# Finishing four more output tiles straight from PSUM on VectorE, with a new order of instructions

## The chip, the cores and the metric

The kernel runs on one core of a Trainium2 chip. The metric is device time in microseconds. Before the change it is 129.96 us, the median of three runs (129.57 to 130.26).

## The reference

The input `x` has 2048 rows (s) of 512 columns (d), in bfloat16. Two branches are computed from it and mixed by a gate, row by row:

```python
x = A_x
g = _sigmoid((x * gate_w).sum(-1, keepdims=True))
a = irfft2(rfft2(x) * (w_r + 1j * w_i))        # branch A, cast to bfloat16
h = einsum("bsd,df->bsf", x, w1) + b1          # branch B, f = 1792
b = einsum("bsf,fd->bsd", h * tanh(softplus(h)), w2)
return g * a + (1 - g) * b
```

Branch A is a two-dimensional Fourier filter, branch B a dense layer with the Mish activation and a second dense layer. The output has the shape of `x`.

## The kernel before

The 2048 rows are 16 tiles of 128 rows. Branch B runs in four chunks of four tiles. For a chunk, line 795 does 14 groups of four matmuls (128x512) into PSUM, line 811 applies Mish on ScalarE into `act`, and line 830 does 14 matmuls for each tile, in two halves of seven (called `mm2_t_0` and `mm2_t_1`; tile 15 is instead cut into three column pieces of 256, 128 and 128). Branch A is written as matmuls too: the transforms along the columns (line 533) and the rows (line 559), a write to a scratch tensor in HBM and a read back that regroups it (`scr<-Ybuf`, then `Abuf<-scr`), the second row step (line 656), the weights on VectorE and GpSimd (line 414, tiles `Qb` and `Zb`), the inverse row step (line 716), a second trip through scratch, and then, for every one of the 16 tiles, the inverse transforms of lines 744 and 755.

After line 755 a tile t goes through this sequence, which the change and the prediction speak of:

- line 748 (an eviction, in the trace line 409 on VectorE or 410 on ScalarE, tile `Zb`) takes the result of line 744 out of PSUM for line 755;
- `gc_t` on ScalarE (line 760) scales half of the result of line 755 by the gate; `sap_t` and `sam_t` on VectorE (line 766) scale the other half and add or subtract the first, into `Qb`;
- `sbp_t` and `sbm_t` (line 414, `Tg<-Qb`, 128x256 each) add and subtract these and leave the gated branch A in `ga`, which is the tile `Tg`. They run on GpSimd for tiles 0 to 13, and on either engine for 14 and 15;
- for tiles below `NBF`, `bev_t` evicts the second dense layer from PSUM, scaled by 1 - g (line 776 on ScalarE, line 777 on VectorE), into `xo`, and `sum_t` (line 414, `xo<-xo,Tg`, 128x512 in bfloat16) adds `ga` on VectorE. Two tiles go out in one store of 256 KB;
- for the other tiles `fin_t` (line 842) does both in one VectorE instruction: it reads PSUM, scales by 1 - g and adds `ga`. Each such tile, and each piece of tile 15, has its own store.

A PSUM bank comes free when its last reader is done. With `bev_t` that reader needs only the matmuls and the gate; with `fin_t` it needs `ga` of that tile as well.

Nothing is scheduled at run time and nothing by a cost rule: `_Graph.schedule` reads the string `ORDER`. It gives, in one list for the whole kernel, the number of the next task, the engine where a task has a choice, and the PSUM bank where a task takes one. Each engine executes its tasks in that order, and waits on semaphores for what a task depends on. So an instruction that waits holds up everything behind it on its engine. Stores and loads are issued by SyncE (the SP queue) unless the call names another queue; the first store on SyncE waits for the landing of all loads and scratch transfers. `ORDER` numbers the tasks as they are created, so other tasks mean other numbers throughout.

Of the kernel before, what the change touches and what calls it, by code (L numbers as in the profile page):

```python
# [165 lines left out]
class _Graph:  # L166
# [97 lines left out]
    "2wv2xv2l2Qa88252R22ca8n0802ya8d4262e2z52nv2Sv2U2mv3C8e2oa8Z7372p22T2qv2d30a3J8a7X17Z68r731328j48x58t23E2s7Y398"
    "f38u8p18y7a8b28o3B3G2r0f7s50e3D7j08s8c7t3I3F0t3H3K3O8h63P77k3Q3R8k3S8q3L3T3Y18g3X33W3Z3U3hv8i3M3gv7p73kv8v67q3"
    "jg8133N7uv8w3ig823a7m47la3b3lv3V3c63ng3t24F03d3e3u542v0w3f3mg7n3o3v7ra43v45g3w8N746v8O7oa3x44g47v48g3y249g3p33"
    "z4H4Ov9Z28Pa8Q73ra4Pv4Qg4G03qa4b34Tv4I4Rg9a9R54J9D69N29S404d9E4K54Sv9X08R4lv414L4A4kv4c54Ug9O9Y4Vg4e4B04M8Sa4C"
    "a4N9P44f4pv8W74W4ov8z54g64mg4ng4Da4X04h8T64rg3s904Zv4qg4i4j9J54s4Ya4t04E9Q4ua8U4vv4a9H49V09T19F28Va943959K9W9I"
# [696 lines left out]
```

## Time and profile before

| What | us |
|---|---|
| median of three runs | 129.96 |
| the profiled execution | 129.91 |
| its span (first to last instruction in the trace) | 128.2 |
| PE busy (TensorE matmuls) | 122.0 |
| DVE busy (VectorE) | 88.3 |
| ACT busy (ScalarE) | 71.4 |
| POOL busy (GpSimd) | 56.5 |

The profiled execution is the one that all durations below come from; it lies 0.05 us under the median, and 1.7 us of its time lie outside the span. PE, PEld (weight loads), DVE, ACT and POOL are the engines; SPq is SyncE's queue, ACTq the queue of ScalarE. In a row of the profile `out<-in` names the tiles, `x14` the number of instructions, and ns is the mean of one. The granted TensorE clock is full speed in this run.

### The profile page before, as it was taken

The page shows a single profiled execution, that of the slowest core. Times are in us where ns is not written, and L with a number is a line of the kernel's source. Part 1 is how long each engine was busy: PE and PEld are TensorE (multiplying, and loading weights), DVE is VectorE, ACT ScalarE, POOL GpSimd, SP SyncE. Part 2 cuts the span into 40 slices and gives each one's busy share as a digit, 9 for nine tenths or more (in the row PEclk, how much of TensorE's full clock was granted, in tenths as well). Part 3 has the DMA queues.
Part 4 walks back from the last instruction along what each step waited for, and adds up shares of the span by engine and source line. Part 5 has one row for each costly group of instructions (what it writes and reads, how often), then busy time and mean ns, then how long its engine had stood idle before and what let it go on. Part 6 is the DMA issues. An engine that isn't in the chain of part 4 may idle for free.

```text
span 128.2 us, 2701 instructions
## 1 busy us (share of the span) xinstructions
PE 122.0 (95%) x998; PEld 66.6 (52%) x1014; DVE 88.3 (69%) x175; ACT 71.4 (56%) x122; POOL 56.5 (44%) x90
## 2 busy tenths in 40 slices
PE   7999989999999999999999999999999999999970
PEld 5786445535644444444544444444457667555570
DVE  0258999897999940179787975430007979999992
ACT  1326595989988087204329455664348895955100
POOL 4000047000000045248899989700000899999930
PEclk9999999999999999999999999999999999999999
DMA  3999937599999767991000501463396000200645
GB/s 72 352 401 392 208 92 219 162 311 160 217 300 303 233 178 220 343 407 37 0 0 8 164 0 44 135 203 117 67 345 245 0 5 3 82 0 5 226 183 164
DMA packets 19293, 21.16 MB, mean 165 GB/s; under 512 B 1744, under 2 KB 15952, under 8 KB 19152
## 3 DMA queue, kind: packets, MB, share of 16 engines
q1 hardware_dynamic: 18176, 19.67, 51.4%
q10 hardware_dynamic: 816, 0.79, 1.8%
q0 software_dynamic: 288, 0.53, 1.5%
q8 instruction: 8, 0.13, 0.5%
q14 instruction: 5, 0.04, 0.1%
HBM read 13.64 MB, written 6.29 MB: 156 GB/s over the span
## 4 chain that ended last, share of the span: by engine, by line
PE 82%; DVE 13%; issue 2%; DVEq 0%; ACT 0%
PE ps L795 38%; PE ps L830 26%; DVE Qb L766 5%; DVE xo L414 5%; PE ps L430 3%; PE ps L533 3%; PE ps L559 3%; PE ps L744 2%; PE ps L716 2%; PE ps L481 2%; PE ps L755 2%; PE ps L656 2%; DVE Tg L414 1%; DVE xo L842 1%; DVE Zb L409 0%
## 5 line engine op out<-in xcount | busy, mean ns | idle before, releaser
L795 PE MATMUL ps<-xT,w_sb 128*128 128x512 bf16 (+1 forms) x237 | 53.0, 366 | 0.6 <-issue 0.3
L830 PE MATMUL ps<-w_sb,act 128*128 128x512 bf16 (+2 forms) x240 | 49.8, 354 | 0.8 <-issue 0.3
L811 ACT ACTIVATE act<-ps,b1f 128x512 bf16<-128x512 f32 x56 | 35.8, 690 | 21.0 <-PE ps L795 16.7
L830 PEld LDWEIGHTS ps<-w_sb,act 128*128 128x128 bf16 x252 | 22.8, 98 | 22.7 <-issue 0.6
L795 PEld LDWEIGHTS ps<-xT,w_sb 128*128 128x128 bf16 x240 | 22.5, 98 | 22.9 <-issue 1.4
L414 POOL TENSOR_TENSOR Tg<-Qb 128x256 bf16<-128x256 f32 x29 | 22.5, 808 | 17.8 <-DVE Qb L766 17.8
L414 POOL TENSOR_TENSOR Zb<-Qb 128x510 bf16<-128x510 f32 x16 | 19.9, 1268 | 3.1 <-DVE Qb L414 2.9
L414 DVE TENSOR_TENSOR Qb<-ps,WT 128x1024 f32<-128x1024 f32 x16 | 18.9, 1211 | 1.1 <-PE ps L656 1.1
L766 DVE SCALAR_TENSOR_TENSOR Qb<-ps,gcol,Qb 128x256 f32<-128x256 f32 x32 | 13.7, 474 | 1.7 <-ACT Qb L760 1.5
L776 ACT ACTIVATE xo<-ps,omg 128x512 bf16<-128x512 f32 x12 | 8.1, 686 | 11.0 <-PE ps L830 8.5
L580 POOL TENSOR_TENSOR gcol<-omg,gdot 128x16 f32<-128x16 f32 x1 | 2.9, 2943 | 24.7 <-DVE Tg L575 24.7
L414 DVE TENSOR_TENSOR Abuf<-ps,Tg 128x512 bf16<-128x512 f32 x16 | 10.3, 684 | 2.4 <-ACT Tg L540 2.0
L410 ACT ACTIVATE Ybuf<-ps 128x1024 bf16<-128x1024 f32 x10 | 10.0, 1021 | 2.2 <-PE ps L716 1.7
L575 DVE SCALAR_TENSOR_TENSOR Tg<-xo,Tg 128x512 bf16<-128x512 bf16 x16 | 10.5, 684 | 0.3
L409 DVE CAST Zb<-ps 128x512 bf16<-128x512 f32 x4 | 2.6, 680 | 11.6 <-PE ps L744 11.6
L379 POOL DMA_DIRECT2D xT<-act x8 | 4.0, 507 | 14.9 <-DVE act L489 14.9
L409 DVE CAST Ybuf<-ps 128x1024 bf16<-128x1024 f32 x6 | 7.3, 1221 | 2.8 <-PE ps L716 2.2
L760 ACT ACTIVATE Qb<-ps,gcol 128x256 f32<-128x256 f32 x16 | 7.1, 476 | 3.7 <-PE ps L755 3.5
L414 DVE TENSOR_TENSOR xo<-xo,Tg 128x512 bf16<-128x512 bf16 x14 | 8.7, 644 | 0.0
L410 ACT ACTIVATE Zb<-ps 128x512 bf16<-128x512 f32 x12 | 6.7, 594 | 2.1 <-PE ps L744 2.1
L409 DVE COPY xT<-ps 128x512 bf16<-128x512 bf16 (+1 forms) x5 | 2.6, 528 | 5.8 <-PE ps L481 5.8
L540 ACT ACTIVATE Tg<-ps 128x512 f32<-128x512 f32 x8 | 4.6, 599 | 2.5 <-PE ps L533 2.2
(62 smaller groups left out, 87.4 us busy)
## 6 DMA issues: line engine op xcount, KB each, us to landing
Abuf<-scr SPq DMA_DIRECT2D x8, 512.0 KB, 6.6
scr<-Ybuf SPq DMA_DIRECT2D x16, 128.0 KB, 3.8
scr<-Ybuf SPq DMA_DIRECT2D x4, 512.0 KB, 2.9
w_sb<-in_B_w_dram SPq DMA_DIRECT2D x2, 896.0 KB, 8.5
out_dram<-xo SPq DMA_DIRECT2D x7, 256.0 KB, 2.1
xo<-in_A_x_dram SPq DMA_DIRECT2D x3, 512.0 KB, 7.4
rt<-c_rt SPq DMA_DIRECT2D x2, 512.0 KB, 7.5
WT<-in_A_w_r_dram SPq DMA_DIRECT2D x7, 128.5 KB, 6.8
```

The source lines that it names most:

```text
L379: t = G.add(name, queue, issue if issue != 0.62 or queue != "pool" else 1.0, lambda e: e.dma_start(dst, src), reads=reads, writes=writes, ...
L409: fs = {"dve": ("dve", dve_dur(n, rate=rate), lambda e: e.tensor_copy(out=dst(), in_=src())), "act": ("act", act_dur(n), lambda e: e.activ ...
L410: "act": ("act", act_dur(n), lambda e: e.activation(dst(), src(), AF.Copy))}
L414: f = lambda e: e.tensor_tensor(out=o(), in0=i0(), in1=i1(), op=op)
L540: G.add(f"eg_{t}", "act", act_dur(512), lambda e, gb=gb, pa=pas[0], pv=pv: e.activation(G0[:, gb].rearrange("p t c (m s) -> p t c m s", s= ...
L575: lambda e, t=t: e.scalar_tensor_tensor(out=junk[t % 2], in0=xo[:, t, :], scalar=1.0, in1=gwb, op0=ALU.mult, op1=ALU.mult, accum_out=gdot[ ...
L760: lambda e, t=t, sl=sl, p5=p5: e.activation(gC[:, sl, :].rearrange("p (i n) -> p i n", i=2), ps[:, p5.bank, :].rearrange("p (i n) -> p i n ...
L766: lambda e, t=t, sl=sl, p5=p5, o=o, op=op: e.scalar_tensor_tensor(out=st1[:, sl, o::2, :], in0=ps[:, p5.bank, :].rearrange("p (i n) -> p i ...
L776: G.add_multi(f"bev_{t}", [("act", act_dur(512, True), lambda e: e.activation(xo[:, t, :], ps[:, pd.bank, :], AF.Copy, scale=omg[:, t:t + ...
L795: ins = e.matmul(o if c < 2 else o.rearrange("p (a t j) -> p a t j", a=4, t=4), w1_sb[:, i, 128 * ft:128 * (ft + 1)], xTp[:, i, 512 * c + ...
L811: lambda e, c=c, ft=ft, pd=pd, hb=hb: e.activation(act[:, hb, ft, :].rearrange("p (t a j) -> p t a j", t=4, a=4), ps[:, pd.bank, :].rearra ...
L830: ins = e.matmul(ps[:, pd.bank, cs_], act[:, hb, ft, 128 * tl:128 * (tl + 1)], w2_sb[:, ft, cs_], start=(ft == 0), stop=(ft == NFT - 1))
```

## The change

`NBF` falls from 14 to 10. Tiles 10, 11, 12 and 13 so lose their eviction `bev_t` and their sum `sum_t`; each gets one `fin_t` instead, and a store of 128 KB of its own in place of half of a 256 KB store. The stores of tiles 13 and 14 are issued by ScalarE's queue instead of SyncE's. The whole string `ORDER` is replaced: other order on all five engines, other PSUM banks, and other choices of engine where a task has two.

```diff
 ORDER = (
-    "0M0N0420506070P080O090A0B0U0C00010Q0D0R0E020F0G0H0I0x00yv0J0K0L0T0z30S10v037F27511151347A314v1X67K70V7B12a1Y7G"
+    "0M0450P05060708090N0A0B000C0D0U0E010O0F0G0H0I0x10yv0J0K0Q0z20L10v0R7K37501140S12v1357F6027A77G14v7L7B761Zv7C7D"
...
 )
-NBF = 14
+NBF = 10
 SHQ = ("pool", "sp", "pool", "sp")
...
                     dma(f"out{t}{part}", ov[:, t, cs_], xo[:, t, cs_], reads=[("o", t, part)],
-                        nbytes=256 * (cs_.stop - cs_.start), is_out=True, prio=PR["fin"], tail=0.6)
+                        nbytes=256 * (cs_.stop - cs_.start), is_out=True, prio=PR["fin"], tail=0.6, queue="act" if t in (13, 14) else "sp")
```

The number of matmuls is the same. Two places are shown in their order, since the next section rests on them.

The end of VectorE's program. L766 are `sap_t` and `sam_t`, `xo<-xo,Tg` the sums, `Tg<-Qb` the `sb` additions, `Zb<-ps` the evictions ahead of line 755, and L842 the `fin` instructions. First before:

```order
L766 SCALAR_TENSOR_TENSOR Qb<-ps,gcol,Qb 128x2x128 x6
L414 TENSOR_TENSOR xo<-xo,Tg 128x512 x4
L766 SCALAR_TENSOR_TENSOR Qb<-ps,gcol,Qb 128x2x128 x3
L414 TENSOR_TENSOR xo<-xo,Tg 128x512
L766 SCALAR_TENSOR_TENSOR Qb<-ps,gcol,Qb 128x2x128
L414 TENSOR_TENSOR Tg<-Qb 128x2x128 x3
L842 SCALAR_TENSOR_TENSOR xo<-ps,omg,Tg 128x512
L414 TENSOR_TENSOR xo<-xo,Tg 128x512 x2
L842 SCALAR_TENSOR_TENSOR xo<-ps,omg,Tg 128x256
L842 SCALAR_TENSOR_TENSOR xo<-ps,omg,Tg 128x128 x2
```

So three `Tg<-Qb` additions, tile 14 and the sums of tiles 13 and 12 stand just ahead of tile 15's pieces. And the same place now, still on VectorE:

```order
L842 SCALAR_TENSOR_TENSOR xo<-ps,omg,Tg 128x512
L766 SCALAR_TENSOR_TENSOR Qb<-ps,gcol,Qb 128x2x128
L414 TENSOR_TENSOR xo<-xo,Tg 128x512
L766 SCALAR_TENSOR_TENSOR Qb<-ps,gcol,Qb 128x2x128 x2
L414 TENSOR_TENSOR Tg<-Qb 128x2x128
L414 TENSOR_TENSOR xo<-xo,Tg 128x512
L766 SCALAR_TENSOR_TENSOR Qb<-ps,gcol,Qb 128x2x128 x2
L414 TENSOR_TENSOR xo<-xo,Tg 128x512
L842 SCALAR_TENSOR_TENSOR xo<-ps,omg,Tg 128x512
L766 SCALAR_TENSOR_TENSOR Qb<-ps,gcol,Qb 128x2x128 x2
L842 SCALAR_TENSOR_TENSOR xo<-ps,omg,Tg 128x512 x2
L842 SCALAR_TENSOR_TENSOR xo<-ps,omg,Tg 128x256
```

Behind the last row shown stand `fin_13` (128x512) and the two 128x128 pieces of tile 15. Two of the three `Tg<-Qb` additions on VectorE have gone to GpSimd, which has 31 of them at its end instead of 29, with `sbp_13` and `sbm_13` (tile 13's) last. The two `fin` in one row are those of tiles 11 and 12.

SyncE's queue between the regrouped loads (`xT<-act`) and the first read of scratch (`Abuf<-scr`). `WT` are the filter weights, `w_sb` here the halves of `w2`. Before:

```order
L379 DMA w_sb<-in_B_w_dram 128x7x512
L379 DMA WT<-in_A_w_i_dram 16x4112 x2
L379 DMA WT<-in_A_w_r_dram 16x4112
L379 DMA scr<-Ybuf 64x4x256
L379 DMA WT<-in_A_w_i_dram 16x4112 x2
L379 DMA scr<-Ybuf 64x4x256 x15
L379 DMA WT<-in_A_w_r_dram 16x4112
L379 DMA WT<-in_A_w_r_dram 16x16x257
L379 DMA rt<-c_rt 128x2048
L379 DMA Abuf<-scr 128x2048 x4
```

Here both halves of `w2` (the other stands further ahead) are issued ahead of all 16 writes to scratch. Now:

```order
L379 DMA scr<-Ybuf 64x4x256 x4
L379 DMA WT<-in_A_w_i_dram 16x4112
L379 DMA w_sb<-in_B_w_dram 128x7x512
L379 DMA WT<-in_A_w_i_dram 16x16x257
L379 DMA WT<-in_A_w_r_dram 16x257
L379 DMA scr<-Ybuf 64x4x256 x2
L379 DMA WT<-in_A_w_i_dram 16x4112 x2
L379 DMA scr<-Ybuf 64x4x256
L379 DMA WT<-in_A_w_r_dram 16x4112
L379 DMA scr<-Ybuf 64x4x256 x9
L379 DMA WT<-in_A_w_i_dram 16x4112
L379 DMA WT<-in_A_w_r_dram 16x4112
```

The same 16 writes and the same loads stand ahead of the read; four writes now stand ahead of the second half of `w2`, and the last weight load ahead of the read has 16 rows of 4112 elements instead of 256 rows of 257.

More of the change, by code (lines that the diff above doesn't have):

```diff
@@ L264 @@
[L264 to L268, printed above, removed]
@@ new lines @@
+    "7M771av1X1031l27H0T1m47R51Y3J0V781711n7V21ov1pv18v0W0X1A1547E1qa1c1797W7P71C0Y7S0b7T016v7N8947I7Q1b27J1G7O191E"
+    "1B8F51d0a0c1F1D1K1wv8G8A7v78360Z1N1S1T1vv8L51R273347w2821O1ev8D47U29841fv8B78M1x01ga1W1z873361L8E1y1331H2Av1r5"
+    "381U1M8J01I7f41J8C881sa2Bv20v2Cv21v1Q1V7h38K1h61P2D17x53A3C2Ea2Jv7b022a2Hv7y2318H52Iv7i2Kv2V31iv8560d2W77c8x00"
+    "e0l8I24v2gv2M10u0s2X2fv2hv2iv0p2Yv2Zv2L20g350i8l30n2G1u2u57g1k862t41t0k2av2N8m2v2Ov8y2Pv7Z62k72wv0v2Qa2b20r2j4"
+    "2xv0j7z17a2yv2l7d02nv1j2z5252mv2ca80370o0q2R22ov8r48d730a26392Sv2p52qv3B8s0h2F8p17X43E8q8j28f38k2e8g3D2d323181"
@@ new lines @@
+    "57Y2T8t68h17e2U3F8u2r8b23G2s8e0m828Z33I7j40f0t8a3H7p03K7s58c8i3O3P67t3Q3T3L3X23M3Y63R3N7q3S3hv3V7ra3gv3a7k3Z3W"
+    "3U7m13kv3b8n03jg3lv3c73t27la3ig7ua3mg4F48o3d3u67n43v42v8N03v3ng46v8v23w45g0w9T347v3e9Z64H8O44g4Ov4Pv8w7oa3x3y7"
+    "9a3f4G19U48g3o3z8Pa49g3p38Q74I3ra4Tv403qa9R04Rg4J4b34Qg4Sv414c54K14kv4Ug4L9J24d4e9S9K4A4M4N9P04Vg4W4lv8R4f4ov4"
+    "B19Q8z04pv3s8Sa9X74g54Da9F64ng4Cv4X1904mg4qg4h9404i4E4j8W54s4Ya9Y9G4rg4Zv4t14vv4ua8X959f79164a9b38Ya4w9V19W96v"
+    "9L58T24x9M9c9g8U9d45P55H05139e52a9H15Qv5974y5R48Va5Iv5S5v55334z5Av5n25T5U5J05wa9775B55K5oa5L545M505Wg9I5C5X45x"
@@ L274 @@
+    "2565Vg55925Og5p05E5Ng5y57g5Ya5D6315zA6v6J393a5f55Z45q986B658g6Kv5ga5Fg6L35r5s5h55a5c64a6R05ug6Sa6065161gA2v6M9"
+    "B2A5v5tg6T06Cv5b5Gg6O5i6Z66NA79N4A3v6aa5dg5k5j62g6p36Qg6h66U6V6qa5eg5lg9C6r55mg6D3666W9O6b0A46Yg6iaABv67ACv9p4"
+    "6s6EA8v686j69q6Pg6x16G6F9h36ya6u996z79l19m9i6t6c6Ag69g6k6Ig9t5AEv706e6d6vvA9v6Hg6Xg729A719w09z7AFv6wg6ggAD6fg9"
+    "r73gAA6m74g6l9D9j6og9EAG9u6ng9n9xA09s9v9o9k9yA1"
 )
-NBF = 14
+NBF = 10
 SHQ = ("pool", "sp", "pool", "sp")
```

9 lines of the change are left out of this document (removed).

## The prediction

> **What bounds the kernel now.** I read the page first (busy shares and the chain of waits), then the busy time by stretch, then the end of the span in order of time.
>
> ```profile
> span 128.2 us, 2701 instructions
> PE 122.0 (95%) x998; PEld 66.6 (52%) x1014; DVE 88.3 (69%) x175; ACT 71.4 (56%) x122; POOL 56.5 (44%) x90
> PE 82%; DVE 13%; issue 2%; DVEq 0%; ACT 0%
> ...
> 54.70:95.50 40.80, 40.22 (x420) 18.97 (x427) 23.15 (x33) 19.92 (x28) 24.07 (x38) 1.00 0.34 112
> 95.50:116.50 21.00, 20.84 (x190) 13.40 (x192) 18.13 (x40) 15.23 (x32) 16.10 (x22) 1.00 0.16 62
> 116.50:124.30 7.80, 7.75 (x66) 4.99 (x63) 7.80 (x15) 1.87 (x4) 6.38 (x8) 1.00 0.46 170
> 124.30:128.20 3.90, 0.00 (x0) 0.00 (x0) 1.43 (x5) 0.00 (x0) 0.00 (x0) 1.00 0.42 135
> ```
>
> In the lines by stretch the columns are length, busy PE, PEld, DVE, ACT, POOL, granted clock, DMA share and GB/s. PE is busy in 7.75 of the last 7.80 us before 124.30, and nearly as full earlier, at full clock. The change takes no matmul away, so PE cannot end much before 124.30. What is left to win is the 3.9 us behind it, and a few tenths of PE waits; what can be lost is any new wait of PE, at one to one. The end in order of time, from timelines, a group of stores, and the stores by size (KB and us from issue to landing):
>
> ```profile
> 110.05 12.82 POOL L414 TENSOR_TENSOR Tg<-Qb 128x256 bf16<-128x256 f32 x16 [0.28 <-DVE Qb L766]
> 116.51 7.79 PE L830 MATMUL ps<-w_sb,act 128*128 128x512 bf16 x62
> 118.22 0.69 ACT L776 ACTIVATE xo<-ps,omg 128x512 bf16<-128x512 f32 x1 [0.54 <-PE ps L830]
> 121.74 1.76 DVE L414 TENSOR_TENSOR Tg<-Qb 128x256 bf16<-128x256 f32 x3
> 123.42 0.74 DVE L842 SCALAR_TENSOR_TENSOR xo<-ps,omg,Tg 128x512 bf16<-128x512 f32 x1
> 124.08 0.74 DVE L414 TENSOR_TENSOR xo<-xo,Tg 128x512 bf16<-128x512 bf16 x2
> 124.74 0.99 DVE L842 SCALAR_TENSOR_TENSOR xo<-ps,omg,Tg 128x256 bf16<-128x256 f32 x3
> 126.19 0.45 SPq L379 DMA_DIRECT2D out_dram<-xo  x1
> L379 SPq DMA_DIRECT2D out_dram<-xo x7: 332/412/450, 121.4 to 126.2; - x7
> out_dram<-xo SPq DMA_DIRECT2D x1, 128.0 KB, 1.7
> out_dram<-xo SPq DMA_DIRECT2D x2, 32.0 KB, 1.6
> ```
>
> PE ends at 116.51 + 7.79 = 124.30, ScalarE at 118.91, GpSimd at 122.87, VectorE at 125.73. VectorE is late: three additions and three 128x512 instructions stand ahead of tile 15's pieces, whose matmuls are done. SyncE issues the last seven stores one by one, 412 ns each at the median, so the last goes out at 126.19, 0.46 after VectorE's end. From there to the end of the span is 128.2 - 126.19 = 2.0 us (1.6 of it until the data have landed).
>
> **The change part by part.** The durations for VectorE and GpSimd, from the groups in the stretch from 95.5 on and from single tiles (the three numbers behind a colon are shortest, median, longest in ns):
>
> ```profile
> L766 DVE SCALAR_TENSOR_TENSOR Qb<-ps,gcol,Qb 128x256 f32<-128x256 f32 x32 | 13.7, 474 | 1.7 <-ACT Qb L760 1.5 <-PE ps L830 0.2
> L414 DVE TENSOR_TENSOR xo<-xo,Tg 128x512 bf16<-128x512 bf16 x14 | 8.7, 644 | 0.0
> L409 DVE CAST Zb<-ps 128x512 bf16<-128x512 f32 x4 | 2.6, 680 | 11.6 <-PE ps L744 11.6
> L414 DVE TENSOR_TENSOR Tg<-Qb 128x256 bf16<-128x256 f32 x3 | 1.8, 637 | 0.0
> L777 DVE TENSOR_SCALAR xo<-ps,omg 128x512 bf16<-128x512 f32 x1 | 0.7, 740 | 0.0
> L842 DVE SCALAR_TENSOR_TENSOR xo<-ps,omg,Tg 128x512 bf16<-128x512 f32 x1 | 0.7, 739 | 0.0
> L414 DVE TENSOR_TENSOR xo<-xo,Tg x14: 407/636/944, 104.6 to 124.4; 128x512 bf16<-128x512 bf16 x14
> L414 DVE TENSOR_TENSOR xo<-xo,Tg x2: 409/410/412, 124.1 to 124.4; 128x512 bf16<-128x512 bf16 x2
> L766 DVE SCALAR_TENSOR_TENSOR Qb<-ps,gcol,Qb x32: 468/474/484, 98.3 to 121.3; 128x256 f32<-128x256 f32 x32
> L414 POOL TENSOR_TENSOR Tg<-Qb x29: 721/732/972, 99.3 to 122.0; 128x256 bf16<-128x256 f32 x29
> L414 POOL TENSOR_TENSOR Tg<-Qb 128x256 bf16<-128x256 f32 x29 | 22.5, 808 | 17.8 <-DVE Qb L766 17.8
> ```
>
> A sum takes 409 to 412 ns once GpSimd is done and up to 944 while it works; GpSimd's additions stretch from 721 to as much as 972. Line 766, which has one input in PSUM, stays at 468 to 484 all through. The Trainium skill, SBUF — State Buffer, section "Who interferes with whom", says that a VectorE instruction with both inputs in SBUF and a GpSimd instruction that reads SBUF exclude each other. By that rule, the trace agrees, with 944 against 409.
>
> *VectorE.* `fin` also reads one input from PSUM. Its 739 was taken with GpSimd idle; stretched as the sums are (944 - 409 = 535) it would be 1274. I take 739, because line 766 beside a busy GpSimd did not stretch. The sums that stay: at 407 to 944 each. The last two of the 14 stand behind GpSimd's end (409 and 412 ns); the other twelve share 14 x 644 - 821 = 8195, or 683 each, and I take 683 for the ten. So from 95.5 on: sums 10 x 683 - 14 x 644 = -2.19 us; four `fin` at 739, +2.96; two `Tg<-Qb` given to GpSimd, -1.27; the one L777 eviction, which in the new list stands ahead of the `Zb` casts, in the 11.6 us in which VectorE waits, -0.74; one `Zb` cast more, +0.68; two instructions fewer, each of which overlaps its neighbour by 0.08, +0.16. Sum -0.4 (ends -3.2 and +4.4, from 407 for each sum and from 944 with 1274 for each `fin`).
>
> VectorE also begins earlier. It waits for the first results of line 744:
>
> ```profile
> 95.55 1.06 PE L744 MATMUL ps<-GMs,Abuf 128*128 128x128 bf16 x16
> 96.65 1.29 DVE L409 CAST Zb<-ps 128x512 bf16<-128x512 f32 x2 [11.61 <-PE ps L744]
> ```
>
> The 16 matmuls are four tiles, some 0.22 us apart. Before, VectorE's first cast takes the fourth; the new table gives it the first, so 3 x 0.22 = 0.7 earlier. PE has as much work ahead of that point in both lists (between the last L716 group and the first L744 group, five halves of L830 and five groups of L795 in each). The 1.7 us in which line 766 waits for ScalarE can vanish or stay; I take half, 0.85. VectorE's own work would then end at 125.73 - 0.4 - 0.7 - 0.85 = 123.8. But its last piece needs PE's last matmul: 124.30 and 0.34 for the piece, and a few hundredths for the signal, 124.7. So PE would bound it.
>
> *GpSimd.* It runs from 99.27 to 122.87, idle for 1.1 of these:
>
> ```profile
> 99.27 1.41 POOL L414 TENSOR_TENSOR Tg<-Qb 128x256 bf16<-128x256 f32 x2 [16.64 <-DVE Qb L766]
> ```
>
> The other gaps are 17.8 - 16.6. Two additions more, at 0.69 after overlap, +1.4. The stretch was 29 x (808 - 732) = 2.2 us for 17 VectorE instructions of the conflicting kind; 11 are left, -0.8. Of the 1.1 idle, 0 to 0.6 goes, since VectorE feeds it more steadily: -0.3. So GpSimd ends at 122.87 + 0.3 = 123.2 (122.9 to 123.8). `fin_13` needs its last addition, and the two last pieces stand behind it: 123.25 + 0.66 + 0.26 + 0.34 = 124.5, still under 124.7; with 123.8 it is 125.1.
>
> *Stores.* SyncE's last four are now a piece of tile 15, tile 12 and two pieces. The three pieces wait for VectorE, so there is no queue of older stores left: the last piece goes out 0.3 after VectorE's end or sooner, at 125.0 instead of 126.19. The stores of tiles 13 and 14 move to ScalarE, past its last work (118.91 before); that queue's issue costs 0.65 here, from
>
> ```profile
> 0.80 1.95 ACTq L379 DMA_DIRECT2D w_sb<-in_B_w_dram  x3
> ```
>
> and tile 13's, with `fin_13` ending at 123.25 + 0.74 = 124.0, would land at 124.1 + 1.7 = 125.8, ahead of the last piece (125.0 + 1.6 = 126.6). Two more stores of 128 KB cost nothing as long as they go out ahead of that.
>
> ScalarE loses three evictions of 0.69 us, which it did in time that nobody waited for; if its waits stay the same, nothing is gained there.
>
> *The rest of the order.* One place ahead of the tail has no slack: the first read of scratch.
>
> ```profile
> 29.62 2.08 SPq L379 DMA_DIRECT2D WT<-in_A_w_i_dram  x2
> 34.38 5.73 SPq L379 DMA_DIRECT2D scr<-Ybuf  x7
> 47.93 1.79 SPq L379 DMA_DIRECT2D Abuf<-scr  x4
> 54.69 0.35 PEld L656 LDWEIGHTS ps<-Abuf,rt 64*32 64x32 bf16 x32 [0.42 <-DMA Abuf<-scr]
> ```
>
> PE waits 0.42 for it. SyncE issues DMA after DMA up to that read, some 0.65 each; in two places (2.08 for two, 5.73 for seven) an issue took about 1 us longer. The new list has the same number ahead of it. Better by more than 0.42 it cannot get; one such long issue more costs 1.0, two 2.0. I take nothing, since the count is the same.
>
> **The sum.** The last store 1.2 us earlier (126.19 to 125.0), the 2.0 behind it unchanged, PE unchanged: 129.91 - 1.2 = 128.7; I give 0.1 back for small waits of PE in a wholly new order: 128.8. The profiled execution lies 0.05 under the median, so this is a median too.
>
> **The rivals.**
>
> *Late scratch (slower).* Four scratch writes now stand ahead of the second half of `w2` and wait for evictions of lines 409 and 410, with all that follows. Each microsecond by which the read comes later is one for PE and for the end. From 1.2 it eats the gain; from 1.85 the kernel is slower by over 0.5%. With two long issues more and a wait, 2.2: 130.9. For it: no slack. Against it: same transfers, same count. 12%.
>
> *PE waits for a bank.* With `fin` the accumulators of tiles 10 to 13 stay in PSUM until the gated branch A of that tile is done. Tile 10's bank goes next to tile 15's group of line 755, ahead of which VectorE has `fin_10` in the middle of its list, and behind which PE has the last three halves of L830 and tile 15, as before the change (7.79 us). If VectorE is 1 us late there, PE ends 1 us later: 129.8. For it: VectorE is full (7.80 of 7.80). Against: the list gives `fin_10` room. 10%.
>
> *The sum was the cheaper instruction.* The Trainium skill, VectorE: DVE Perf Modes, section "Why PSUM operands drop a tier", speaks against the change: an input in PSUM keeps VectorE from its fastest modes. In the rows, a sum alone takes 410 and `fin` 739: at 410 for the four that go, VectorE's work grows by 4 x 0.33 = 1.3 where I have it at -0.4 (four sums at 410 out, the other ten unchanged at 738: -1.64 + 2.96 - 1.27 - 0.74 + 0.68 + 0.16 = +0.15). With the idle time also unchanged, VectorE ends at 125.73 + 0.15 - 0.7 = 125.2 and the last store at 125.5: 129.2; with GpSimd at its late end too, 129.4. For it: the last two sums did take 410. Against it: most of the 14 did not. 14%.
>
> **How the numbers follow.** My forecast, VectorE's tail shortened to PE's end, has 64%. About 0.5% (0.65 us) is what a measurement can tell from no change. Faster: the forecast, 64%, with most of it under 129.2. Same: the cheap sum, 14%, and the bank wait, 8 of its 10%. Slower: the late scratch, 12%, and a bank wait of over 1.9 us, 2%. The range runs from 128.2 (forecast, and the 0.42 at the scratch read gone as well) to 130.0, which takes in the bank wait and the cheap sum and leaves the late scratch out.
>
> **What would show it.** Right: PE ends within 0.3 of 124.3; GpSimd has 31 additions and ends near 123.2; four more L842 of 128x512 at about 740 beside a busy GpSimd; VectorE ends 0.4 to 0.5 after PE; the last store leaves near 125.0. Wrong: a wait of PE on `Abuf<-scr` above 1 us, idle PE ahead of line 755 in the tail, `fin` near 1270, or the last landing being ScalarE's store.

## The result, and the profile after

The changed kernel takes 128.92 us (median of 20 runs, 127.8 to 132.7) against 129.87 us for the kernel before, run beside it (median of 20, 129.24 to 131.33). The ratio is 0.9914, with a 95% interval from 0.9888 to 0.9941: faster by 0.9%, where 0.5% can be told from no change. Forecast were 128.8 us and 128.2 to 130.0. The ratio takes in the runs within 1.5% of each kernel's fastest, 15 of 20 with a median of 128.65 us and 19 of 20 with one of 129.84; the other five of the changed kernel took 129.87 to 132.71. So the runs of the changed kernel differ more among themselves than those of the kernel before; the experiments say a part of why.

The profiled execution of the changed kernel took 129.21 us, 0.3 over its median; 1.8 us lie outside its span. From the page (span, busy shares, and the engines' shares of the chain that ended last):

```profile
span 127.4 us, 2711 instructions
PE 122.2 (96%) x999; PEld 67.0 (53%) x1014; DVE 91.0 (71%) x176; ACT 67.4 (53%) x115; POOL 57.0 (45%) x92
PE 90%; DMA 6%; issue 1%; DVE 0%
```

Before, the chain that ended last was 82% PE and 13% VectorE. VectorE has gone from it (0%); what stands beside PE now is a DMA. The timeline, at the first scratch read and at the end:

```profile
47.37 0.34 SPq L379 DMA_DIRECT2D Abuf<-scr  x1
...
55.22 0.35 PEld L656 LDWEIGHTS ps<-Abuf,rt 64*32 64x32 bf16 x32 [1.12 <-DMA Abuf<-scr]
55.23 0.63 PE L656 MATMUL ps<-Abuf,rt 64*32 64x256 bf16 x32 [0.63 <-DMA Abuf<-scr]
...
117.28 7.57 PE L830 MATMUL ps<-w_sb,act 128*128 128x512 bf16 x62
...
122.16 3.08 DVE L842 SCALAR_TENSOR_TENSOR xo<-ps,omg,Tg 128x512 bf16<-128x512 f32 x6
122.32 1.41 POOL L414 TENSOR_TENSOR Tg<-Qb 128x256 bf16<-128x256 f32 x2 [0.25 <-DVE Qb L766]
...
124.89 0.90 SPq L379 DMA_DIRECT2D out_dram<-xo  x2
```

PE ends at 117.28 + 7.57 = 124.85, VectorE at 122.16 + 3.08 = 125.24, which is 0.39 behind PE, and GpSimd at 123.73. SyncE's last two issues fill 124.89 to 125.79; the last of them starts at 125.33, 0.09 behind VectorE's end. Before, that last issue started at 126.19, 0.46 behind VectorE's end and 1.89 behind PE's. VectorE and GpSimd from 95.5 on, grouped (us in all and mean ns, then idle time ahead), and in a second fence the sums alone with shortest, median and longest ns:

```profile
L766 DVE SCALAR_TENSOR_TENSOR Qb<-ps,gcol,Qb 128x256 f32<-128x256 f32 x32 | 13.7, 474 | 0.4
L414 DVE TENSOR_TENSOR xo<-xo,Tg 128x512 bf16<-128x512 bf16 x10 | 7.4, 761 | 0.0
L842 DVE SCALAR_TENSOR_TENSOR xo<-ps,omg,Tg 128x512 bf16<-128x512 f32 x5 | 3.6, 737 | 0.0
L409 DVE CAST Zb<-ps 128x512 bf16<-128x512 f32 x5 | 3.4, 687 | 8.6 <-PE ps L744 8.6
...
L414 POOL TENSOR_TENSOR Tg<-Qb 128x256 bf16<-128x256 f32 x31 | 23.4, 787 | 17.2 <-DVE Qb L766 17.1
```

```profile
L414 DVE TENSOR_TENSOR xo<-xo,Tg x10: 415/844/947, 102.7 to 120.0; 128x512 bf16<-128x512 bf16 x10
```

The single instruction takes 737 ns beside a busy GpSimd, as it did alone. The idle time of line 766 has gone from 1.7 to 0.4 us. The ten sums that stay are not cheaper than before but dearer (761 against 644).

**One mark to measure from.** PE's first L656 group, which reads the scratch, starts at 54.69 before and at 55.23 after. Before:

```profile
54.69 0.63 PE L656 MATMUL ps<-Abuf,rt 64*32 64x256 bf16 x32
```

PE's end lies 69.61 us behind it before and 69.63 after. In twelve of the fourteen traces of this study (five of the old order, seven of the new) PE's end is 69.61 to 69.63 behind that mark; the other two are the old order with the single instruction, told of below. So the mark splits a run in two: what happened ahead of it, which differs from trace to trace (the mark lies at 54.0 to 54.7 us in the old order and at 53.6 to 56.1 in the new), and the end, where PE's path is the same to a few hundredths. By the mark, before and after:

| us behind the first L656 matmul | before | after |
|---|---|---|
| PE's end | 69.61 | 69.63 |
| VectorE's end | 71.04 | 70.02 |
| last store issued | 71.50 | 70.10 |
| end of the span | 73.5 | 72.2 |

The end is 1.3 us shorter. The medians of all runs differ by only 0.95, those of the runs in the ratio by 1.2. So a median run of the changed kernel seems to lose 0.1 to 0.3 us ahead of the mark; this is a difference of medians and is read from no single trace.

### The profile page after: what moved, and what is told of

Same layout as the page of the kernel before. It is cut to its first block, busy times and chain, and to the rows that moved or that the text cites. A ratio compares the mean times of both kernels' runs of the same rounds, so it can differ in the third digit from the quotient of the medians.

```text
span 127.4 us, 2711 instructions
## 1 busy us (share of the span) xinstructions
PE 122.2 (96%) x999; PEld 67.0 (53%) x1014; DVE 91.0 (71%) x176; ACT 67.4 (53%) x115; POOL 57.0 (45%) x92
## 4 chain that ended last, share of the span: by engine, by line
PE 90%; DMA 6%; issue 1%; DVE 0%
PE ps L795 37%; PE ps L830 33%; DMA Abuf<-scr 6%; PE ps L430 3%; PE ps L533 3%; PE ps L744 3%; PE ps L755 3%; PE ps L559 3%; PE ps L481 2%; PE ps L656 2%; PE ps L716 2%; DVE xo L842 0%; PE ps L673 0%; PE ps L499 0%; PE ps L675 0%
## 5 line engine op out<-in xcount | busy, mean ns | idle before, releaser
L830 PE MATMUL ps<-w_sb,act 128*128 128x512 bf16 (+2 forms) x242 | 49.8, 354 | 1.0 <-issue 0.6
L830 PEld LDWEIGHTS ps<-w_sb,act 128*128 128x128 bf16 x252 | 22.7, 98 | 22.7 <-issue 0.8
L414 POOL TENSOR_TENSOR Tg<-Qb 128x256 bf16<-128x256 f32 x31 | 23.4, 787 | 17.2 <-DVE Qb L766 17.1
L766 DVE SCALAR_TENSOR_TENSOR Qb<-ps,gcol,Qb 128x256 f32<-128x256 f32 x32 | 13.7, 474 | 0.4
L409 DVE CAST Ybuf<-ps 128x1024 bf16<-128x1024 f32 x7 | 8.6, 1222 | 4.3 <-PE ps L716 3.8
L410 ACT ACTIVATE Ybuf<-ps 128x1024 bf16<-128x1024 f32 x9 | 9.2, 1032 | 4.6 <-PE ps L716 3.5
L776 ACT ACTIVATE xo<-ps,omg 128x512 bf16<-128x512 f32 x9 | 6.1, 686 | 10.1 <-PE ps L830 9.9
L409 DVE CAST Zb<-ps 128x512 bf16<-128x512 f32 x5 | 3.4, 687 | 8.6 <-PE ps L744 8.6
L414 DVE TENSOR_TENSOR xo<-xo,Tg 128x512 bf16<-128x512 bf16 x10 | 7.4, 761 | 0.0
```

The source lines that it names most:

```text
L409: fs = {"dve": ("dve", dve_dur(n, rate=rate), lambda e: e.tensor_copy(out=dst(), in_=src())), "act": ("act", act_dur(n), lambda e: e.activ ...
L410: "act": ("act", act_dur(n), lambda e: e.activation(dst(), src(), AF.Copy))}
L414: f = lambda e: e.tensor_tensor(out=o(), in0=i0(), in1=i1(), op=op)
L766: lambda e, t=t, sl=sl, p5=p5, o=o, op=op: e.scalar_tensor_tensor(out=st1[:, sl, o::2, :], in0=ps[:, p5.bank, :].rearrange("p (i n) -> p i ...
L776: G.add_multi(f"bev_{t}", [("act", act_dur(512, True), lambda e: e.activation(xo[:, t, :], ps[:, pd.bank, :], AF.Copy, scale=omg[:, t:t + ...
L830: ins = e.matmul(ps[:, pd.bank, cs_], act[:, hb, ft, 128 * tl:128 * (tl + 1)], w2_sb[:, ft, cs_], start=(ft == 0), stop=(ft == NFT - 1))
```

## The experiments

In the expectations for the old order the mark was put at the second L656 group, 0.23 us later; all figures below are from the first. In kernels with an inserted line the numbers of later lines are a few higher (L657 and L658 are L656).

**Does the single instruction carry the gain?** First the new order with evictions and sums back:

```
-                    G.add(f"fin_{t}_{part}", "dve", ...)
+                    if t in (10, 11, 12, 13):
+                        evict_b(t, pd)                  # on ScalarE
+                        tt(f"sum_{t}", ..., engs=("dve",))  # where fin stood
+                    else:
+                        G.add(f"fin_{t}_{part}", "dve", ...)
```

> The changed kernel in its new order, but tiles 10 to 13 again take an eviction (on ScalarE, as soon as the matmuls are done) and a sum on VectorE where the single instruction stood. My theory (order and queue carry the gain): sums beside a busy GpSimd take as long as the single instruction (761 against 737 ns), so nothing moves: ratio to before 0.990 to 0.993. Rival (the single instruction carries the gain): ratio 0.997 or more. Second rival (ScalarE's four evictions of 0.69 us delay what VectorE waits for): 0.3 to 0.7 us slower than the changed kernel, with idle time of line 766 behind ScalarE back at over 1 us.

Measured: 128.54 us, ratio 0.990 (0.9873 to 0.9928). Timeline:

```profile
54.28 0.63 PE L657 MATMUL ps<-Abuf,rt 64*32 64x256 bf16 x32
...
116.34 7.57 PE L831 MATMUL ps<-w_sb,act 128*128 128x512 bf16 x62
...
124.47 0.46 SPq L380 DMA_DIRECT2D out_dram<-xo  x1
```

PE ends at 123.91 (69.63 behind the mark) and the last store goes out at 124.47 (70.19, against 70.10 with the single instruction). Nothing is lost without it.

My rival in the prediction was that the sum is the cheaper instruction, since a sum alone takes 410 ns and the single instruction 739. The Trainium skill has a rule for this (VectorE: DVE Perf Modes, "Why PSUM operands drop a tier"): an input in PSUM keeps VectorE from its fastest modes. It decided nothing here. The four sums of tiles 10 to 13 in this run:

```profile
113.98 0.54 DVE L415 TENSOR_TENSOR xo<-xo,Tg 128x512 bf16<-128x512 bf16 x1
...
121.42 1.28 DVE L415 TENSOR_TENSOR xo<-xo,Tg 128x512 bf16<-128x512 bf16 x2
...
123.31 0.43 DVE L415 TENSOR_TENSOR xo<-xo,Tg 128x512 bf16<-128x512 bf16 x1 [0.22 <-POOL Tg L415]
```

They took 536, 410, 945 and 426 ns, 2.3 us against 2.9 for four single instructions, so on VectorE they were the cheaper form. The 0.6 us does not arrive: in both kernels VectorE's last piece waits for PE's last matmul and ends 0.39 behind it. Beside a busy GpSimd much of a sum's advantage goes: the ten sums of the changed kernel take 761 ns in the mean and up to 947. The Trainium skill, SBUF — State Buffer, "Who interferes with whom", says for two inputs in SBUF that they contend with a GpSimd instruction that reads SBUF. My expectation (the same time either way, because a sum takes as long as the single instruction) was right in the time and wrong in the reason.

Then the old order with the single instruction put where the sums stood:

```
-                    if t < NBF or (t < NT - 1 and part == 0):
+                    if (t < NBF and t not in FIN) or (t < NT - 1 and part == 0):
...
-                if t < NBF:
+                if t < NBF and t not in FIN:
                     evict_b(t, pd)
```

with `FIN = (10, 11, 12, 13)`, sums of these tiles left out of the list, and PSUM banks assigned anew.

> The kernel before, every engine in its old order, but tiles 10 to 13 finished by one L842 instruction at the places where their sums stood (their evictions go; PSUM banks are reassigned so that PE need not wait; stores as before). My theory (the order and the stores carry the gain, the single instruction as such is worth nothing): the last two sums took 410 ns each behind GpSimd's end and become 740 each, so VectorE's tail grows by 0.66 us, less 0.2 for the sum of tile 10 that took 944; the kernel comes out 0.3 to 0.7 us slower than before, near 130.4. Rival (the single instruction carries the gain): 0.5 to 1.0 us faster, near 129.1.

Measured: 130.39 us, ratio 1.0069 (1.0035 to 1.0102). The waits of the run, then its timeline:

```profile
PE ps L745 <- DVE Qb L767: 1.0, 1, 1.0
```

```profile
54.56 0.63 PE L657 MATMUL ps<-Abuf,rt 64*32 64x256 bf16 x32
...
117.89 7.79 PE L831 MATMUL ps<-w_sb,act 128*128 128x512 bf16 x62
...
125.74 1.80 SPq L380 DMA_DIRECT2D out_dram<-xo  x4
```

Slower by what I expected, but not only for my reason. Tile 11's accumulator, held until `fin_11`, keeps the bank that tile 11's L744 group had before; the groups behind it move to other banks, and tile 15's L744 group gets one that VectorE has not yet read empty, so PE waits 1.0 us. PE ends at 125.68, 71.1 behind the mark instead of 69.6. (0.3 of these 1.5 us are there already at the first L744 matmul.) That is my rival of the bank wait, in the place of another tile. So the same without tiles 11 and 13, `FIN = (10, 12)`, whose accumulators are filled only behind that place:

> As the run before, but only tiles 10 and 12 take the single L842 instruction; with two accumulators held instead of four, no PSUM bank has to be reused early (PE waited 1.0 us for one at L744 in the run with four). My theory: PE has no new wait; the sum of tile 10 (944 ns) becomes 740, that of tile 12 (410 ns, behind GpSimd's end) becomes 735, so VectorE's end and the last store come 0.1 to 0.3 us later, measured from the first L656 matmul in the trace (71.27 us before); ratio 1.000 to 1.003. Rival (the bank wait was harmless and the single instruction itself cost the half microsecond): 0.4 us or more later, ratio 1.004 or more. Second rival (the single instruction saves time where no bank is short): 0.3 us earlier, ratio 0.997.

Measured: 129.76 us, ratio 1.0003 (0.9977 to 1.003). Timeline:

```profile
54.19 0.63 PE L657 MATMUL ps<-Abuf,rt 64*32 64x256 bf16 x32
...
123.88 1.65 DVE L843 SCALAR_TENSOR_TENSOR xo<-ps,omg,Tg 128x512 bf16<-128x512 f32 x4
```

No wait of PE at tile 15's L744 group is left. VectorE's end is at 125.53, 71.3 behind the mark, 0.3 later than before. Half of this is not the single instruction's: PE is 0.15 later from the first L744 matmul on, and so is its end. The other 0.15 is the single instruction's price at the end of the old order, where a sum runs behind GpSimd's end at 410 ns; and for tile 11 it holds a PSUM bank that the old order needs. It is worth nothing in the new one.

**Is the queue of stores the gain?** The old order, with the stores of tiles 12 and 13 (one transfer) and 14 in ScalarE's queue:

```
-    dma(f"out{t}", ..., is_out=True, prio=PR["fin"], tail=0.6)
+    dma(f"out{t}", ..., is_out=True, prio=PR["fin"], tail=0.6, queue="act" if t == 13 else "sp")
...
-    dma(f"out{t}{part}", ..., is_out=True, prio=PR["fin"], tail=0.6)
+    dma(f"out{t}{part}", ..., is_out=True, prio=PR["fin"], tail=0.6, queue="act" if t == 14 else "sp")
```

> The kernel before with nothing changed but the queue of two stores: those of tiles 12 and 13 (one store) and tile 14 go out in ScalarE's queue. My theory: SyncE then holds only the three pieces of tile 15 at the end, and the last piece goes out at VectorE's end plus 0.1 to 0.2 (125.85 to 125.95) instead of 126.19, so 0.2 to 0.35 us are gained, near 129.6. Rival (the queue of stores was the whole loss at the end): 0.8 to 1.0 us gained, near 129.0. Second rival (the end hangs on VectorE alone): nothing, 129.87.

Measured: 129.75 us, ratio 0.9999 (0.9974 to 1.0024). My 0.2 to 0.35 is not there. Timeline:

```profile
54.37 0.63 PE L656 MATMUL ps<-Abuf,rt 64*32 64x256 bf16 x32
...
124.44 0.99 DVE L842 SCALAR_TENSOR_TENSOR xo<-ps,omg,Tg 128x256 bf16<-128x256 f32 x3
124.94 1.46 SPq L379 DMA_DIRECT2D out_dram<-xo  x3
```

Tile 15's first piece ends at 124.9 and SyncE takes it at once. The other two follow at the queue's own pace, and the last goes out at 125.81: 71.44 behind the mark, 0.06 better than before. Three pieces that come out of VectorE in 1 us take SyncE 1.46 us, whatever else has left its queue.

The same two stores put back into SyncE's queue in the new order:

```
-   ..., tail=0.6, queue="act" if t in (13, 14) else "sp")
+   ..., tail=0.6)
```

> The changed kernel with only the stores of tiles 13 and 14 put back into SyncE's queue, at the places that the order gives them. My theory: SyncE must issue tile 13's store when its last instruction ends (124.6), then tile 12's and the two last pieces at 0.4 us each, so the last goes out near 125.8 instead of 125.33: 0.3 to 0.5 us slower than the changed kernel, a ratio to before of about 0.995. Rival (the queue is worth nothing, since VectorE's last piece sets the end): same as the changed kernel, ratio 0.991. Second rival (the queue is the whole gain): ratio 1.00.

Measured: 129.46 us, ratio 0.9975 (0.9934 to 1.0017). Timeline:

```profile
54.19 0.63 PE L656 MATMUL ps<-Abuf,rt 64*32 64x256 bf16 x32
...
121.14 3.07 DVE L842 SCALAR_TENSOR_TENSOR xo<-ps,omg,Tg 128x512 bf16<-128x512 f32 x6
...
121.90 3.76 SPq L379 DMA_DIRECT2D out_dram<-xo  x8
```

VectorE ends at 124.21, 70.02 behind the mark, exactly as with ScalarE's queue. But eight stores stand back to back on SyncE for 3.76 us, and the last goes out at 125.22, 1.0 behind VectorE's end. By the mark the span ends 0.8 later than in the changed kernel; the medians differ by 0.54, or by 0.64 for the runs in the ratios (129.29 and 128.65). I had expected 0.3 to 0.5. The intervals of the two ratios just overlap, so the size rests on the traces. In the new order the queue is worth what it was not worth in the old.

**Two limits side by side.** To see that in the old order, VectorE's end is relieved without any of the change's means, by leaving the sums of tiles 10 to 13 out:

```
+            if t not in (10, 11, 12, 13):
                 tt(f"sum_{t}", ...)
```

> The kernel before with the four sums of tiles 10 to 13 left out and nothing in their place (these tiles' outputs lack branch A's part): what it is worth, at most, to free VectorE at the end. My theory (VectorE's tail bounds the end before, PE behind it): VectorE's own work shrinks by 944 + 452 + 410 + 410 ns less 0.3 of overlap, 1.9 us, but its last piece must follow PE's end by 0.4, so the end moves by 1.0 to 1.4 only; 128.5 to 128.9, ratio 0.989 to 0.993, PE's end 69.4 us behind the first L656 matmul as before. Rival (PE's work or the stores bound already): 0.0 to 0.3 gained. Second rival (VectorE alone bounds, without PE close behind): 1.9 gained, 128.0.

Measured: 128.97 us, ratio 0.9936 (0.9906 to 0.9966). Timeline:

```profile
54.29 0.63 PE L657 MATMUL ps<-Abuf,rt 64*32 64x256 bf16 x32
...
122.52 1.77 DVE L843 SCALAR_TENSOR_TENSOR xo<-ps,omg,Tg 128x512 bf16<-128x512 f32 x4
...
124.62 0.95 SPq L380 DMA_DIRECT2D out_dram<-xo  x2
```

VectorE ends at 124.29, 0.39 behind PE and 70.00 behind the mark, as in the changed kernel. Of VectorE's 1.0 us only 0.7 arrives, where I had expected 1.0 to 1.4: SyncE's last issue is at 125.13, 0.84 behind VectorE. Now both, the sums left out and the two stores in ScalarE's queue:

> The kernel before with the sums of tiles 10 to 13 left out (branch A's part is missing in these tiles' outputs) and the stores of tiles 12 and 13 and of tile 14 in ScalarE's queue: both reliefs of the end together. The queue alone gave nothing, the sums alone 0.9. My theory (two limits lie side by side, VectorE's list and SyncE's stores, and each relief shows only when the other limit is gone too): the last store goes out 70.0 to 70.2 us behind the first L656 matmul instead of 70.6 (sums alone) and 71.2 (queue alone), 128.4 to 128.7, ratio 0.988 to 0.991. Rival (the stores don't matter in the old order): as with the sums alone, 128.97, ratio 0.9936.

Measured: 128.8 us, ratio 0.9925 (0.9886 to 0.9964). Timeline:

```profile
54.60 0.63 PE L657 MATMUL ps<-Abuf,rt 64*32 64x256 bf16 x32
...
122.83 1.77 DVE L843 SCALAR_TENSOR_TENSOR xo<-ps,omg,Tg 128x512 bf16<-128x512 f32 x4
...
124.86 0.46 SPq L380 DMA_DIRECT2D out_dram<-xo  x1
```

The last store goes out at 70.26 behind the mark, against 70.84 with the sums alone, 71.44 with the queue alone and 71.50 before. The traces show the queue's 0.6 at the last issue once VectorE is out of the way, of which 0.4 reaches the end of the span (72.4 against 72.8). The medians of these two kernels (128.97 and 128.8) are too close for their intervals to tell apart; this point rests on the traces.

**Is VectorE full in the changed kernel?** Tile 15's two additions go back from GpSimd to VectorE:

```
 GpSimd:  ... sbp_12, sbm_12, -sbm_15, -sbp_15, sbp_13, sbm_13
 VectorE: ... sam_15, sap_15, +sbm_15, +sbp_15, sum_9, fin_14, sam_13, sap_13, ...
```

> The changed kernel with two of GpSimd's 31 additions (tile 15's) given back to VectorE, ahead of the sum of tile 9. My theory (VectorE is full up to PE's end in the changed kernel): VectorE gets two instructions of 0.41 to 0.85 us, so its end moves by 0.7 to 1.5 less what GpSimd's earlier end gives back (sums at 410 instead of 842 to 944): 0.3 to 0.9 us slower than the changed kernel, ratio to before 0.994 to 0.999; in the trace VectorE's end is 0.7 to 1.3 us behind PE's instead of 0.39. Rival (PE bounds with room to spare, or GpSimd does): no change, ratio 0.991.

Measured: 129.1 us, ratio 0.9943 (0.9913 to 0.9973), 0.2 over the changed kernel's median of all runs and 0.4 over that of the runs in its ratio; the intervals overlap, so the trace decides. In the profiled execution of this kernel the scratch read went out 2.1 us late (49.48 instead of 47.37), and it took 1.7 us more than the kernel's median; the end is therefore read from the mark:

```profile
56.10 0.63 PE L656 MATMUL ps<-Abuf,rt 64*32 64x256 bf16 x32 [1.48 <-DMA Abuf<-scr]
...
118.16 7.57 PE L830 MATMUL ps<-w_sb,act 128*128 128x512 bf16 x62
...
123.71 2.96 DVE L842 SCALAR_TENSOR_TENSOR xo<-ps,omg,Tg 128x512 bf16<-128x512 f32 x6
123.87 1.41 POOL L414 TENSOR_TENSOR Tg<-Qb 128x256 bf16<-128x256 f32 x2 [2.48 <-DVE Qb L766]
```

VectorE ends at 126.67, 0.94 behind PE (70.57 by the mark instead of 70.02), and the span ends 0.7 later by the mark. GpSimd, with two additions fewer, waits 2.48 us for VectorE's tile 13 and ends later than with them. VectorE is full nearly up to PE's end in the changed kernel: there its last piece, which waits for PE, starts 0.03 us behind the one ahead, where pieces that wait for nothing overlap by 0.08, so some 0.1 us is left. Moving these additions to GpSimd, worth 0.55 at VectorE's end, is part of what brought that end from 71.04 to 70.02.

The late read in this trace bears on the prediction. SyncE's list is the same as in the changed kernel up to there; the first four writes to scratch took SyncE, in the changed kernel and then here:

```profile
28.68 3.18 SPq L379 DMA_DIRECT2D scr<-Ybuf  x4
```

```profile
28.40 4.25 SPq L379 DMA_DIRECT2D scr<-Ybuf  x4
```

The next two took 2.16 us instead of 1.30. So two long issues, 1.9 us together, stand ahead of the late read, and PE waited 1.48 us for the data. That is the late-scratch rival as the prediction has it, in one execution of the new order. Whether the five runs of the changed kernel from 129.87 us up are of this kind no trace shows.

**Why do the runs of the changed kernel differ?** Counted without the wait, PE reaches the first L656 group of the new order at 53.6 to 54.5 us, and it waited there for the scratch read by 0.70, 0.20 and 0.00 us in the traces of the changed kernel, of the one with SyncE's queue and of the one with sums (the idle time of the weight load, 1.12, 0.62 and 0.42, less the 0.42 that it has ahead of that group even where the data are long there). To take the wait away, the load of the table that L656 multiplies by is cut in two; a quarter of it is all that the first two groups need:

```
-        dma("ld_rf", rt[:, 0:2048], d_RT[:, 0:2048], writes=["RF"], nbytes=128 * 4096)
+        dma("ld_rf0", rt[:, 0:512], d_RT[:, 0:512], writes=["RF0"], nbytes=128 * 1024)
+        dma("ld_rf1", rt[:, 512:2048], d_RT[:, 512:2048], writes=["RF1"], nbytes=128 * 3072)
...
-                   reads=[("In2", r, u) for r in range(2)] + ["RF"],
+                   reads=[("In2", r, u) for r in range(2)] + ["RF0" if u < 2 else "RF1"],
 SyncE:  ... ld_Wp02, -ld_rf, +ld_rf0, r1r0, +ld_rf1, r1r2, r1r3, r1r1, ld_ri
```

> The changed kernel with the load of the table that L656 reads cut in two: the quarter that the first two groups need goes out ahead of the first scratch read, the other three quarters (384 KB) right behind it. My theory (in the changed kernel PE reaches the first L656 group before the scratch read has landed, by 0 to 0.7 us in the three traces that I have, and this is what makes its runs differ): the read lands about 0.7 to 1.0 us earlier, the wait of PE ahead of L656 goes, the median falls by 0.2 to 0.4 us to 128.5 to 128.7, ratio to before 0.987 to 0.990. Rival (the runs differ for what happens earlier, in the first loads): same median and spread as the changed kernel, 0.991. Second rival (the three quarters behind delay the other scratch reads): a wait at the L656 groups near 61 us instead, 0.3 to 1.0 us slower.

Measured: 128.47 us, ratio 0.988 (0.9843 to 0.9916), and its six runs lie between 128.22 and 128.64. The first scratch read in the view of transfers (size, then us from issue to landing), before:

```profile
Abuf<-scr SPq DMA_DIRECT2D x1, 512.0 KB, 6.6
```

in the changed kernel:

```profile
Abuf<-scr SPq DMA_DIRECT2D x1, 512.0 KB, 7.8
```

and with the cut load:

```profile
Abuf<-scr SPq DMA_DIRECT2D x1, 512.0 KB, 4.2
```

Timeline of the kernel with the cut load:

```profile
47.38 0.34 SPq L379 DMA_DIRECT2D Abuf<-scr  x1
...
54.53 0.63 PE L657 MATMUL ps<-Abuf,rt 64*32 64x256 bf16 x32
...
124.65 0.46 SPq L379 DMA_DIRECT2D out_dram<-xo  x1
```

Issued at the same time (47.38 and 47.37), the read lands at 51.6 instead of 55.2, and PE meets no wait. The end is unchanged: 124.65 is 70.12 behind the mark. The median is 0.45 us below the changed kernel's of all runs, but only 0.2 below the 128.65 of the runs in its ratio, and the two intervals of the ratio overlap: the wait's end is shown, a gain over the changed kernel is not. That the read makes the runs differ would fit the six runs (0.42 us between fastest and slowest, against 1.8 in those of the changed kernel that enter its ratio). But six runs are few, the fastest of the changed kernel, 127.8, lies below all of them, and with the cut load and SyncE's queue (below) seven runs differ by 1.0 though PE meets no wait in the trace. So something further ahead differs too; what it is stays open.

The same cut in the old order:

> The kernel before with nothing changed but the table's load cut in two. My theory (before, PE reaches the first L656 group 0.2 us or more after the scratch read has landed, since it has more idle time ahead of that point; only the new order brings PE there earlier than the data): the read lands earlier and nobody gains, 129.6 to 129.9, ratio 0.998 to 1.001. Rival (the early read is worth its 0.4 us in any order): 129.4, ratio 0.996 to 0.997.

Measured: 129.99 us, ratio 1.0014 (0.9993 to 1.0035); the read lands earlier there too, 4.9 us from its issue instead of 6.6, and from the mark to the end of the span it is 73.5 as before. Its row among the transfers:

```profile
Abuf<-scr SPq DMA_DIRECT2D x1, 512.0 KB, 4.9
```

So in the old order the read costs nothing: in its seven traces the data are there 0.2 to 2.0 us ahead of PE's first L656 matmul. In the four traces of the new order without the cut load they come 0.2 us ahead of the time at which PE is ready, or up to 1.5 behind. That is mostly the data: PE is ready there at 54.0 to 54.7 us in the old order and at 54.0 to 54.6 in these four traces of the new, while the uncut read lands at 53.1 to 54.5 and at 54.1 to 56.1. On top of the cut load, both halves of the question once more, without the wait's scatter: the stores back in SyncE's queue,

> The changed kernel with the table's load cut in two (so that the scratch read no longer makes its runs differ) and the stores of tiles 13 and 14 back in SyncE's queue: the price of the queue, measured by itself. My theory (the stores stand back to back on SyncE and hold the last piece up): the last store goes out 0.7 to 1.0 us behind VectorE's end instead of 0.1, so 129.0 to 129.4, 0.5 to 0.9 us slower than the run with the cut load (128.47), ratio to before 0.993 to 0.997. Rival (worth at most 0.2, as the lone move in the kernel before suggests): 128.5 to 128.7, ratio 0.988 to 0.990.

and sums instead of the single instruction:

> The changed kernel with the table's load cut in two, and tiles 10 to 13 finished by an eviction and a sum instead of the single instruction. My theory (the single instruction is worth nothing in this order): 128.3 to 128.7, as the run with the cut load (128.47), ratio to before 0.986 to 0.990. Rival (it saved a little that the scatter hid): 128.8 to 129.2. Second rival (the sums are cheaper, as the runs without the cut load hinted, 128.54 against 128.92): 128.0 to 128.2.

Measured: 129.06 us, ratio 0.9937 (0.9911 to 0.9962) with SyncE's queue, and 128.33 us, ratio 0.9895 (0.9869 to 0.9922; four runs) with sums. Timelines of the first and of the second:

```profile
53.60 0.63 PE L657 MATMUL ps<-Abuf,rt 64*32 64x256 bf16 x32
...
120.54 3.07 DVE L843 SCALAR_TENSOR_TENSOR xo<-ps,omg,Tg 128x512 bf16<-128x512 f32 x6
...
121.31 3.75 SPq L379 DMA_DIRECT2D out_dram<-xo  x8
```

```profile
54.45 0.63 PE L658 MATMUL ps<-Abuf,rt 64*32 64x256 bf16 x32
...
124.64 0.45 SPq L380 DMA_DIRECT2D out_dram<-xo  x1
```

With SyncE's queue VectorE again ends 70.02 behind the mark, the span 0.7 later than with ScalarE's; the median is 0.6 later. With sums the last store is at 70.19, and the median is lower by 0.14, which nothing here can tell from zero. These two, the cut load with the single instruction (128.47) and with sums (128.33), have the lowest medians of the study, though the one with sums and without the cut load (128.54) is within 0.1 of the first.

All runs together, by the mark:

| kernel | ratio to before | VectorE's end | last store issued | end of the span |
|---|---|---|---|---|
| before | 1 | 71.04 | 71.50 | 73.5 |
| old order, single instruction, tiles 10 to 13 | 1.0069 | 72.06 | 72.53 | 74.5 |
| old order, single instruction, tiles 10 and 12 | 1.0003 | 71.33 | 71.80 | 73.8 |
| old order, ScalarE's queue | 0.9999 | 71.06 | 71.44 | 73.5 |
| old order, four sums left out | 0.9936 | 70.00 | 70.84 | 72.8 |
| old order, sums left out, ScalarE's queue | 0.9925 | 70.00 | 70.26 | 72.4 |
| old order, cut load | 1.0014 | 71.04 | 71.50 | 73.5 |
| after | 0.9914 | 70.02 | 70.10 | 72.2 |
| after, sums | 0.990 | 70.02 | 70.19 | 72.3 |
| after, SyncE's queue | 0.9975 | 70.02 | 71.03 | 73.0 |
| after, two additions on VectorE | 0.9943 | 70.57 | 70.78 | 72.9 |
| after, cut load | 0.988 | 70.02 | 70.12 | 72.3 |
| after, cut load, SyncE's queue | 0.9937 | 70.02 | 71.01 | 73.0 |
| after, cut load, sums | 0.9895 | 70.02 | 70.19 | 72.4 |

## Why the prediction was right

*The sum.* Forecast was a last store 1.2 us earlier, nothing lost or won ahead of it, and 0.1 given back. By the mark the last store came 1.4 earlier and the span's end 1.3; ahead of the mark a median run lost 0.1 to 0.3. The mechanism, VectorE's and SyncE's lists shortened to PE's end, is right. That the total came out so close, 128.8 against 128.92, is partly luck: two terms are off by 0.1 to 0.3 in opposite directions.

*PE.* Right: its path from the scratch read to its end is unchanged (69.63 against 69.61). "Within 0.3 of 124.3" was missed in the profiled execution (124.85), all of it ahead of the mark.

*VectorE.* The end 0.4 to 0.5 behind PE is right (0.39), the 739 for the single instruction is right (737), its first cast came 0.66 earlier by the mark (0.7 forecast), and of the idle time of line 766 more went than I took (1.3 instead of 0.85). The sums were mis-sized: 683 ns taken, 761 measured, 0.8 us over ten. I took the mean of the twelve that ran beside GpSimd; in the new order more of them run at full conflict (median 844 instead of 636). That the denser lists of both engines are the reason is argued, no run isolates it. With this, and the one `Tg<-Qb` left at 846 ns instead of 637, the sum of the list that I had at -0.4 us comes out at +0.6. So what brings VectorE's end forward in the new order is not less work in all but less waiting: the earlier start, 0.66, and line 766's idle time, 1.3, less a new gap of 0.24 at the `Zb` casts. VectorE's own work therefore left not the 0.9 us of room that I had counted (123.8 against PE's end and a piece, 124.7) but 0.1. That PE's end still came last hid the error. The run with two additions more on VectorE shows how little was left.

*GpSimd.* 31 additions, end forecast at 123.2, which is 68.5 behind the mark; measured 68.5. It was 0.3 us busier than I had it and 0.3 less idle.

*The stores.* The mechanism is right, its size in the old order was not: the queue alone was worth 0.06 by the trace, and a tie in the ratio, where I expected 0.2 to 0.35 from the lone move. The prediction's 1.2 is one term only because both limits were lifted at once: where the new order's last store comes 1.4 earlier, in the old order VectorE's relief alone brings 0.7 (sums left out), the queue alone 0.1, and both together 1.2 (70.26). A store on ScalarE's queue, which I had at 0.65, took 0.34 to 0.36 to issue.

*The scratch read.* Taken as nothing, with a range from -0.42 to +2. The profiled execution of the changed kernel lost 0.7 there, those with SyncE's queue and with sums 0.2 and 0.0, that with two additions on VectorE 1.5. The late-scratch rival named the right place. In the profiled execution of the changed kernel its cause was not there: the read did not go out later (47.37 against 47.93 before); it landed 7.8 us after its issue instead of 6.6, and PE was ready 0.2 earlier. In the trace with two additions on VectorE its cause was there too, with the price that the prediction gave. So an equal count of issues, for which I took nothing here, does not keep the read on time. The 0.42 in the row of before, which I took for a loss that could be won back, was no wait of PE at all: the weight load waited while PE was still in its last L830 matmuls, and PE's own row there shows no gap. The cut load in the old order, which changed nothing, confirms it.

*The other rivals.* The bank wait did not come in the changed kernel; in the old order with tile 11's accumulator held it did, 1.0 us of it. Of the cheaper sum the first half came: in the new order the four sums take 2.3 us of VectorE's time and the four single instructions 2.9. The second half, a later end, did not: VectorE's last piece waits for PE with either form.

## What to carry to other kernels

Where a list of one engine and a queue of stores end within a few tenths of each other, measure each relief on top of the other: alone, the queue was worth nothing at the end of the span here, and 0.4 to 0.8 us once VectorE was out of its way. Anchor the reading of an end at an event from which the bottleneck engine runs with hardly a gap; differences of 0.05 us show there that medians of ten runs cannot tell. Where an instruction is exchanged and the time stays, look whether its price was the same or another engine's end hid the difference. And an idle time in a weight-load row is a loss only if the matmul row beside it has a gap too.

## What was not expected of the hardware

- Taking 384 KB out of the transfers ahead of a 512 KB scratch read brought its landing forward by 3.6 us with the same issue time (7.8 to 4.2 us from issue to landing; 4.3 and 4.1 in the two other kernels with the new order and the cut load, 6.6 to 4.9 in the old order). The four reads of 512 KB land 1.3 us after one another in the old order, so by that pace, an estimate, 384 KB are worth 1.0 us. The table's own load ahead of the read says more: uncut it lands 3.7 us behind the read's issue, its first quarter 1.5 behind, 2.2 earlier (in the old order 3.4 and 1.7, which is all of the read's 1.7). Where the remaining 1.3 us of the new order come from isn't settled.
- Stores issued back to back on one queue cost more than stores alone: eight took 3.76 us (0.47 each) where the kernel before took 0.33 for a store that the queue had been waiting for and 0.41 to 0.45 for one right behind another.
- GpSimd got slower to finish when work was taken from it: with two additions fewer it ended 0.7 us later by the mark, since the engine that got them feeds it.
